# A Fourier mixing layer with a gated MLP: the second sequence chunk half plain and half by seven products, and VectorE's side work dealt out anew

## The chip, the cores and the metric

The kernel runs on 1 core of one Trainium2 chip. The metric is the device time of one execution in microseconds. Before the change it is 672.76 us, the median of 3 runs (672.74 to 672.93).

## What is computed

`x` is 2048 x 512 in fp32. Its rows are normalised, go through a discrete Fourier transform (along the hidden axis, then along the sequence, of which the real part is kept), and the result is multiplied with a gate from an MLP with 1792 hidden units.

```python
xn = _layernorm(x, axis=-1)
a = jnp.einsum("bsd,ed->bse", xn, dft_hid_re)
b = jnp.einsum("bsd,ed->bse", xn, dft_hid_im)
s = jnp.einsum("ts,bse->bte", dft_seq_re, a) - jnp.einsum("ts,bse->bte", dft_seq_im, b)
h = jnp.einsum("bsd,df->bsf", xn, w1) + b1
h = where(h > 0, h, 0) ** 2
g = silu(jnp.einsum("bsf,fd->bsd", h, w2) + b2)
out = x + s * g
```

## The kernel before

**Arithmetic.** An fp32 operand is split into a high and a low half (`split`, lines 141 to 143): ScalarE writes the high half with a copy that rounds (L136), VectorE the rest by a subtraction (L139). A product of two operands is three matmuls, in the order high x high, high x low, low x high (`PASSES`). Products of 2 x 2 blocks are made in two ways. *Plain*: eight block products, with no sums. *Seven products* (a scheme of the Strassen kind, `PRODUCTS`): seven block products, for which both operands need four sums of blocks more, and whose results are put together by seven additions (`closing_of`, on VectorE, L363, after copies by ScalarE of what lies in PSUM).

**Stages.** TensorE works through four in turn. First the sequence transform: 8 chunks of the output's columns, each a loop over 8 pairs `j` of 128 row blocks of `x`; the normalised `x` is the stationary operand (`XC[j]`), the cosine and sine tables `ct` the moving one. Then the hidden transform (Y units, `wd`), the first MLP layer (H units, `w1`), and the second with the gate and the output. A step of the first stage is one pair of one chunk, written (c, j).

**Chunks 0 and 1 are plain** (`PLAIN = 2`, `products`, lines 388 to 399): per pair 24 matmuls of 512 columns (`pq_b...` in the profile). Chunk 0 normalises `x` as it goes. Chunks 2 to 7 use seven products (`mm`, lines 377 to 384): per step 42 matmuls of 256 columns (`m`, L382), in seven banks of PSUM.

**A step's operand.** For step n, `u` is the raw table (512 KB, three buffers, loaded by SP, L293). VectorE makes four sums in it with three instructions (`sums_b`, L304 to L306); then `g`, one of two buffers, is written by the split: ScalarE's high half as soon as TensorE has finished the step before last, VectorE's low half behind it. In the code of step n stand, in this order, its matmuls, the sums of step n+2, the split of step n+1, the load of step n+4, then closings of the chunk before (`LATER`) and jobs (`EARLY`, `go`, lines 406 to 414). This is the order in which each engine gets its instructions.

**Jobs.** While the first stage runs, the engines also prepare later weights: `d0` to `d3` are the parts of `wd` (raw load into `pq00`, sums, split of 768 elements and then of 1024, each stored to DRAM), `v0`, `v1`, `v6` are parts of `w1`, `p...` are loads of prepared weights, `y...` early operands of the next stage. For the stationary side, `sums` folds the normalised `x` (four instructions of 1024 elements per half of the pairs, L275), and `split_sums` and `split_s1` split the sums into `XC`. Before, this ran beside chunk 1 (`aside`, `beside`), with a budget of 3.6 us per pair.

**The end of a chunk.** ScalarE copies product 1 and then products 7, 5 and 3 out of PSUM (`left`), so that the next chunk may use those banks; VectorE makes the first two closings at once and the others in later steps.

**Hidden units.** In an H unit ScalarE seeds regions of PSUM with negated copies (`seed`, L146), and applies bias, relu and square. For the units in `ACT_PAIR` ScalarE also does the relu and the square of the lower half (L848 and L879); for the others VectorE does it (L860 and L875).

Of the kernel before, what the change touches and what calls it, by code (L numbers as in the profile page):

```python
# [22 lines left out]
PLAIN = 2  # L23

ASIDE = 3.6

SIDE = {7: 1}
# [22 lines left out]
LATER = {0: 1, 1: 1, 2: 2, 4: 1}  # L50
# [44 lines left out]
ACT_PAIR = (4, 5, 6, 8, 10, 12, 14, 16, 18, 21, 25)  # L95
# [9 lines left out]
A11, A21, A12, A22, S2, S3, S4 = range(7)  # L105
S1 = A21

# [23 lines left out]
def fnet_gated_kernel(ctx, tc, x, xt, ct, wd, w1, w2, b1, b2, out):  # L131
# [122 lines left out]

    def ln_hi(j, h):

        nc.vector.tensor_scalar(XC[j][:, 2 * h:2 * h + 2, HI, :], halves(xr[j][:, h]), stats[:, 0, h, j:j + 1],
                                stats[:, 1, h, j:j + 1], op0=ALU.subtract, op1=ALU.mult)

    def xc_parts(j, h):  # L260
        s = slice(2 * h, 2 * h + 2)
        return XC[j][:, s, HI, :], XC[j][:, s, LO, :], halves(xn32[j][:, h])

    s1 = {}

    def sums(g):


        s = xn32[ND * g, "tile"].rearrange("p j h (b n) -> p j (h b) n", b=2)
        t = s1[g] = buf(f"pq1{g}", [P, ND, CW], f"s1_{g}")  # L270
        for to, a, b, op in ((t, s[:, :, 1], s[:, :, 3], ALU.subtract),
                             (s[:, :, 1], s[:, :, 1], s[:, :, 0], ALU.subtract),
                             (s[:, :, 0], t, s[:, :, 0], ALU.subtract),
                             (s[:, :, 2], s[:, :, 2], s[:, :, 0], ALU.add)):
            nc.vector.tensor_tensor(to, a, b, op=op)  # L275
            yield 1.2

    def split_sums(j):
        s = xn32[j].rearrange("p h (b n) -> p (h b) n", b=2)
        split(XC[j][:, S2:S4 + 1, HI, :], XC[j][:, S2:S4 + 1, LO, :], s[:, 0:3])  # L280
        return 0.9

    def split_s1(j):
        split(XC[j][:, S1, HI, :], XC[j][:, S1, LO, :], s1[j // ND][:, j % ND])
        return 0.4
# [9 lines left out]
    def plain_parts(c, j, hs=slice(0, 2)):  # L295
        if (c, j) not in part:
            part[c, j] = operand_buf("g" + "ab"[j % 2], f"g{c}_{j}", 0 if (c, j) == (PLAIN - 1, NJ - 1) else 3 if j in TURNED else 1, (2, 4, CW))
# [4 lines left out]
    def sums_b(t, r):  # L302

        nc.vector.tensor_tensor(t[:, 0:2], r[:, 0:1].to_broadcast([P, 2, 256]), r[:, 1:3], op=ALU.add)  # L304
        nc.vector.tensor_tensor(t[:, 2], t[:, 1], r[:, 1], op=ALU.add)
        nc.vector.tensor_tensor(t[:, 3], t[:, 2], r[:, 3], op=ALU.add)  # L306

    def sums_a(t, a21, a11_a22, a11, a12, turned=False):

        nc.vector.tensor_tensor(t[:, 0:2], a21.to_broadcast([P, 2, 256]), a11_a22, op=ALU.subtract)  # L310
        if turned:
# [9 lines left out]

    def sums_w1(t, r):
        sums_a(t, r[:, 0:1], r[:, 1:4:2], r[:, 1], r[:, 2], turned=True)
# [31 lines left out]
    def closing_of(part_, ms, room):  # L355
# [4 lines left out]
        for to, m, frm, op in ((C11, 2, C21, ALU.add), (C22, 6, C21, ALU.add), (C21, 7, C22, ALU.subtract),  # L360
                               (C12, 5, C22, ALU.subtract), (C22, 5, C21, ALU.add), (C12, 3, C12, ALU.add),
                               (C21, 4, C21, ALU.subtract)):
            nc.vector.tensor_tensor(part_(to), halves(room.get(m, ms[m])), part_(frm), op=op)  # L363
            yield
# [8 lines left out]
    def some(steps_, n):  # L373
        for _ in range(n):
            next(steps_)

# [9 lines left out]
    accs = [[bank(tag, f"pq0_{tag}") for tag in ("b20", "b21", "bb", "bc")]]  # L386

    def products(c, j, h):

        for passes in [PASSES] if c else [[q] for q in PASSES]:  # L390
            for k in range(ND):
                one_product(c, j, h, k, passes)

    def one_product(c, j, h, k, passes=PASSES):
        for a_, b_ in passes:
            w = XC[j][:, 2 * h + k // 2, a_, k % 2 * P:(k % 2 + 1) * P]
            nc.tensor.matmul(accs[c][k], w, part[c, j][:, b_, 2 * h:2 * h + 2],  # L397
                             start=j == 0 and h == 0 and (a_, b_) == (HI, HI),
                             stop=j == NJ - 1 and h == 1 and (a_, b_) == (LO, HI))

    one, two = slice(0, 1), slice(1, 2)
    steps = [(c, j) for c in range(PLAIN, NC) for j in range(NJ)]
    order = [(c, j) for c in range(PLAIN) for j in range(NJ)] + steps
# [12 lines left out]
    def weight(n, raw_, sums_, to, k, e=None, turn=False):  # L416

        if e:
            e = buf(e, [P, 8, 256], f"{n}rt")
            r, t = e[:, 0:4], e[:, 4:8]  # L420
        else:
            r, t = buf("pq00", [P, 4, 256], f"{n}r"), buf("pq01", [P, 4, 256], f"{n}t")
# [4 lines left out]
        sums_(t, r)  # L427
# [7 lines left out]
    makers["d"] = lambda n: weight(f"wd{n}", wd[n], sums_b, WDD[n], n % 2, "e" if n == 1 else None, True)  # L435
    makers["v"] = lambda n: weight(f"w1{n}", w1[n], sums_w1, W1D[n], 0)
# [59 lines left out]
    junk = bank("b31", "junk")  # L496
# [30 lines left out]
    for h in range(2):  # L527
        products(0, 0, h)
    def run(*names):
        go(*names)  # L530
        return 1.6

    aside = chain(sums(0), (split_sums(j) for j in range(ND)), sums(1), (split_sums(j) for j in range(ND, NJ)),
                  (run(v) for v in ("d0", "d0", "d0", "d1", "d1", "d1")))
    load_c(0, 3)
    load_x(4)
    for j in range(1, NJ):
# [27 lines left out]
        for _ in range(SIDE.get(j, 0)):  # L565
            next(aside)
        for h in range(2):
            products(0, j, h)
# [8 lines left out]
    accs.append([bank(tag, f"pq1_{tag}") for tag in ("b30", "b31", "b32", "ba")])  # L577

    def beside(spent):
        while spent < ASIDE:  # L580
            spent += next(aside, ASIDE)

# [3 lines left out]
    def plain_out(k):  # L586
        to = plain[k // 2].rearrange("p (i m d t) -> p d m i t", i=2, m=2, d=2)[:, k % 2]
        copy(to, accs[0][k].rearrange("p (m i t) -> p m i t", m=2, i=2))

    plain_out(0)  # L590
    plain_out(1)
    beside(1.5)
    plain_out(2)
    plain_out(3)
    for k in range(2):
        nc.sync.dma_start(PQD[0][:, k].rearrange("p k n -> p (k n)"), plain[k])
    for j in range(NJ - 1):
# [12 lines left out]
    step_split(0)  # L610
    step_load(3)
    split_s1(NJ - 2)
    for k in (2, 3):
        one_product(1, NJ - 1, 0, k)
    step_sums(1)
    split_s1(NJ - 1)
    for k, h in ((2, 1), (0, 0), (0, 1), (1, 0), (1, 1), (3, 1)):
        one_product(1, NJ - 1, h, k)
    last = buf("e", [P, 2048], "plain1")

    def last_out(k, op):
        to = last.rearrange("p (h i m d t) -> p h d m i t", h=2, i=2, m=2, d=2)[:, k // 2, k % 2]
        op(to, accs[1][k].rearrange("p (m i t) -> p m i t", m=2, i=2))

    for k, op in ((2, copy), (0, copy), (1, copy)):
        last_out(k, op)


    assert not list(aside)
    closing = None  # L630
    for n, s in enumerate(steps):
        c, j = s
        if j == 0:
# [20 lines left out]
        if j == NJ - 1:  # L654
            e = buf("e", [P, 2048], f"c{c}")
# [575 lines left out]
```

## Time and profile before

| what | us |
|---|---|
| median of 3 runs | 672.76 |
| the profiled execution's own time | 672.81 |
| its span, first to last instruction | 671.0 |
| TensorE (PE) busy | 665.1 (99%) |
| VectorE (DVE) busy | 596.4 (89%) |
| ScalarE (ACT) busy | 380.2 (57%) |
| matmuls of chunks 2 to 7 (L382), 2016 | 228.7 |

The granted clock of TensorE is 1.00. Rows of the timeline read: start, duration, engine, line, operation, output<-input, partitions x elements, count, and in brackets the idle time before it with what ended it. A group's row has, after the bar, busy time and the mean ns of one, then the idle time before. Durations of instructions that follow each other overlap a little at their ends, so work in a row is counted from start to start.

### The profile page before, as it was taken

How to read it: one execution, taken by the hardware profiler on the slowest of the kernel's cores; microseconds unless marked ns; L12 is line 12 of the kernel's file. 1: busy time of each engine (PE TensorE's matmuls, PEld its weight loads, DVE VectorE, ACT ScalarE, POOL GpSimd, SP SyncE). 2: the span in 40 equal slices, each digit the busy share in tenths (PEclk: the TensorE clock that was granted, in tenths of full speed). 3: DMA queues.
4: the chain of work that ended last, by engine and by line, in shares of the span. 5: the costliest groups of instructions: out<-in, count | busy, mean ns of one | idle time of the engine just before them, and what ended most of it. 6: DMA issues, size and time to landing. Idle time of an engine off the chain costs nothing.

```text
span 671.0 us, 13184 instructions
## 1 busy us (share of the span) xinstructions
PE 665.1 (99%) x5437; PEld 646.3 (96%) x5437; DVE 596.4 (89%) x831; ACT 380.2 (57%) x524; POOL 8.8 (1%) x11
## 2 busy tenths in 40 slices
PE   9999999999999999999999999999999999999997
PEld 6888889999999999999999999999999999999997
DVE  7997888999999999899899988977877889999997
ACT  6855664634445454444464557888778865454451
POOL 0000000000000000000000000000000000101010
PEclk9999999999999999999999999999999999999999
DMA  8635497646556774759588558565755866777775
GB/s 292 226 115 206 145 347 269 220 142 224 200 167 226 252 282 162 262 186 346 184 303 278 181 189 317 202 251 205 271 182 198 324 243 214 190 218 190 219 205 156
DMA packets 51739, 150.82 MB, mean 225 GB/s; under 512 B 4960, under 2 KB 19552, under 8 KB 50272
## 3 DMA queue, kind: packets, MB, share of 16 engines
q1 hardware_dynamic: 43568, 129.28, 56.9%
q10 hardware_dynamic: 6208, 18.88, 7.1%
q0 software_dynamic: 1904, 1.84, 1.9%
q8 instruction: 42, 0.69, 0.4%
q14 instruction: 17, 0.14, 0.1%
HBM read 101.98 MB, written 47.99 MB: 223 GB/s over the span
## 4 chain that ended last, share of the span: by engine, by line
PE 96%; DVE 1%; ACT 1%; DMA 0%; issue 0%; ACTq 0%; SPq 0%; DVEq 0%
PE m L382 34%; PE m_o L896 15%; PE r_B L790 13%; PE r_A L790 9%; PE pq_b L397 8%; PE r_C L790 4%; PE r_D L790 4%; PE m_last L896 4%; PE pq_ba L397 2%; PE pq_bc L397 2%; PE pq_bb L397 2%; DVE z L1146 0%; DMA x<-in_x 0%; DVE z L946 0%; ACT h L848 0%
## 5 line engine op out<-in xcount | busy, mean ns | idle before, releaser
L382 PEld LDWEIGHTS m<-g,xc 128*128 128x128 f32 x2016 | 228.6, 188 | 0.1
L382 PE MATMUL m<-g,xc 128*128 128x256 f32 x2016 | 228.7, 276 | 0.0
L136 ACT ACTIVATE g<-u 128x1792 fp32r<-128x1792 f32 (+2 forms) x65 | 99.0, 1523 | 126.9 <-PE m L382 89.0
L139 DVE TENSOR_TENSOR g<-u,g 128x1792 fp32r<-128x1792 f32 (+2 forms) x66 | 116.9, 1772 | 19.8 <-ACT g L136 19.2
L896 PE MATMUL m_o<-w,g 128*128 128x256 f32 x882 | 100.5, 276 | 0.0
L896 PEld LDWEIGHTS m_o<-w,g 128*128 128x128 f32 x882 | 100.3, 188 | 0.0
L136 ACT ACTIVATE g<-hr 128x1792 fp32r<-128x1792 f32 (+2 forms) x31 | 48.2, 1565 | 40.0 <-PE m_o L896 16.8
L790 PE MATMUL r_B<-xT,w 128*128 128x256 f32 x504 | 66.6, 277 | 0.4 <-ACT r_B L146 0.4
L397 PE MATMUL pq_b<-g,xc 128*128 128x512 f32 x240 | 65.2, 391 | 0.4 <-DVE small L247 0.4
L790 PEld LDWEIGHTS r_B<-xT,w 128*128 128x128 f32 x504 | 61.5, 188 | 0.5 <-ACT r_B L146 0.5
L139 DVE TENSOR_TENSOR g<-hr,g 128x1792 fp32r<-128x1792 f32 (+2 forms) x31 | 56.7, 1837 | 2.9 <-ACT g L136 2.8
L397 PEld LDWEIGHTS pq_b<-g,xc 128*128 128x128 f32 x240 | 44.7, 188 | 10.7 <-ACT g L136 0.8
L790 PE MATMUL r_A<-xT,w 128*128 128x256 f32 x336 | 42.8, 276 | 0.0
L790 PEld LDWEIGHTS r_A<-xT,w 128*128 128x128 f32 x336 | 40.2, 188 | 0.0
L790 PE MATMUL r_B<-wdp,yg 128*128 128x256 f32 x288 | 35.8, 277 | 0.0
L304 DVE TENSOR_TENSOR u<-u 128x512 f32<-128x512 f32 x48 | 32.8, 684 | 1.9 <-DMA u<-in_ct 1.9
L790 PEld LDWEIGHTS r_B<-wdp,yg 128*128 128x128 f32 x288 | 34.1, 188 | 0.0
L896 PE MATMUL m_last<-w,g 128*128 128x256 f32 x294 | 33.5, 276 | 0.0
L896 PEld LDWEIGHTS m_last<-w,g 128*128 128x128 f32 x294 | 33.4, 188 | 0.0
L139 DVE TENSOR_TENSOR yg<-yraw,yg 128x1792 fp32r<-128x1792 f32 x13 | 26.2, 2018 | 0.6 <-ACT yg L136 0.6
L136 ACT ACTIVATE yg<-yraw 128x1792 fp32r<-128x1792 f32 x13 | 22.2, 1708 | 5.8 <-DVE yraw L313 5.3
L790 PE MATMUL r_D<-xT,w 128*128 128x256 f32 x168 | 23.6, 276 | 0.0
(192 smaller groups left out, 877.8 us busy)
## 6 DMA issues: line engine op xcount, KB each, us to landing
u<-in_ct SPq DMA_DIRECT2D x63, 512.0 KB, 3.8
hd<-h ACTq DMA_DIRECT2D x28, 512.0 KB, 3.9
hr<-hd SPq DMA_DIRECT2D x28, 512.0 KB, 3.8
wdp<-wdd SPq DMA_DIRECT2D x8, 896.0 KB, 6.5
yraw<-pqd SPq DMA_DIRECT2D x13, 512.0 KB, 5.9
pqd<-c SPq DMA_DIRECT2D x6, 1024.0 KB, 6.3
w<-w1d SPq DMA_DIRECT2D x6, 896.0 KB, 8.2
y<-y ACTq DMA_DIRECT2D x8, 512.0 KB, 5.2
```

Of the source, the lines that this page charges most:

```text
L136: nc.scalar.activation(hi, src, AF.Copy)
L139: nc.vector.tensor_tensor(lo, src, hi.bitcast(F32), op=ALU.subtract)
L304: nc.vector.tensor_tensor(t[:, 0:2], r[:, 0:1].to_broadcast([P, 2, 256]), r[:, 1:3], op=ALU.add)
L382: nc.tensor.matmul(ps[:, d], w[:, a_, d * P:(d + 1) * P], halves(mv(b_)), start=first and d == 0 and (a_, b_) == (HI, HI), stop=last and ( ...
L397: nc.tensor.matmul(accs[c][k], w, part[c, j][:, b_, 2 * h:2 * h + 2], start=j == 0 and h == 0 and (a_, b_) == (HI, HI), stop=j == NJ - 1 a ...
L790: nc.tensor.matmul(self.region(REGION[k]), w, mv, start=i == 0 and k in (1, 7), stop=i == len(ops) - 1, skip_group_check=True)
L896: nc.tensor.matmul(m[:, i * 256:(i + 1) * 256], ready[n][:, a_, H_SLOT[a], i * P:(i + 1) * P], W2[p][:, b_, b], start=p == 0 and i == 0 an ...
```

## The change

Chunk 1 becomes mixed. Its pairs 4 to 7 come first, plain: eight products of 256 columns per pair, added up in four banks, three of which are those of products 2, 4 and 3, and a fourth bank, `Z`. Pairs 0 to 3 follow with seven products into the same banks. One closing is added for `Z` (L371 of the new file, `z`). The sums of `x` are made in place, with four blocks split by one instruction; the slots of `XC` move so that A21, which becomes S1, lies beside the others. The sums for pairs 4 to 7 are split behind steps (1,1), (1,2), (2,0) and (2,1) (`SUMS_AT`). `d0` to `d3`, which ran from chunk 1 to chunk 2, run from the mixed part to chunk 4, and the jobs behind them follow; a weight's three sums are now two jobs instead of one. Closings come one per step. The hidden unit 5 leaves `ACT_PAIR`.

```diff
-PLAIN = 2
-ASIDE = 3.6
-SIDE = {7: 1}
+MIXED = 4, 5, 6, 7
+SUMS_AT = {1: 4, 2: 5, 4: 6, 5: 7}
...
 EARLY = {
-    (2, 0): ("d2",), (2, 1): ("d2",), (2, 2): ("d3",), (2, 4): ("d3",), (2, 5): ("d3",), (2, 6): ("d3",),
...
+    (2, 2): ("d0",), (2, 4): ("d0", "d1"), (2, 5): ("d1",), (2, 6): ("d1",),
...
-LATER = {0: 1, 1: 1, 2: 2, 4: 1}
+LATER = {0: 1, 1: 1, 2: 1, 3: 1, 4: 1}
+LATER_1 = {0: 1, 1: 1, 2: 1, 3: 1, 4: 1, 5: 1}
...
-ACT_PAIR = (4, 5, 6, 8, 10, 12, 14, 16, 18, 21, 25)
+ACT_PAIR = (4, 6, 8, 10, 12, 14, 16, 18, 21, 25)
...
-A11, A21, A12, A22, S2, S3, S4 = range(7)
+A11, A12, A22, S2, S3, S4, A21 = range(7)
...
     def split_sums(j):
         s = xn32[j].rearrange("p h (b n) -> p (h b) n", b=2)
-        split(XC[j][:, S2:S4 + 1, HI, :], XC[j][:, S2:S4 + 1, LO, :], s[:, 0:3])
-        return 0.9
-    def split_s1(j):
-        split(XC[j][:, S1, HI, :], XC[j][:, S1, LO, :], s1[j // ND][:, j % ND])
+        split(XC[j][:, S2:S1 + 1, HI, :], XC[j][:, S2:S1 + 1, LO, :], s)
...
+    def plain_step(j):
+        g = part.pop((1, j))
+        for k, pairs_ in ((2, ((A11, 1), (A12, 3))), (4, ((A21, 1), (A22, 3))), (3, ((A11, 0), (A12, 2))),
+                          (Z, ((A21, 0), (A22, 2)))):
+            if k not in ms:
+                ms[k] = bank("ba" if k == Z else banks(1)[k], f"m{k}_1")
+            for i, (a, q) in enumerate(pairs_):
+                mm(ms[k], XC[j][:, a], lambda b_: g[:, b_, q], j == MIXED[0] and not i, k == Z and j == MIXED[-1] and i == 1)
...
-    steps = [(c, j) for c in range(PLAIN, NC) for j in range(NJ)]
+    steps = [(1, j) for j in range(NJ) if j not in MIXED] + [(c, j) for c in range(2, NC) for j in range(NJ)]
...
+    for i, j in enumerate(MIXED):
...
+        elif i == 2:
+            split(*plain_parts(1, MIXED[3]))
+            split_sums(3)
+            some(side[1], 1)
+            step_sums(0)
+            go("d0", "d0")
+        else:
+            step_sums(1)
+            step_split(0)
+            some(side[1], 1)
+        plain_step(j)
+        load_c(*order[NJ + i + 4])
...
-            if j == max(LATER):
+            if j == max(LATER_1):
                 nc.sync.dma_start(PQD[c - 1].rearrange("p h k n -> p (h k n)"), e)
```

**Where instructions move.** First, VectorE ahead of the first step with seven products. `g` are the operands, named by chunk and pair (`g1_7` is chunk 1, pair 7), `u` the tables, `xn32_4` the `x` of pairs 4 to 7, `xc3` a pair's stationary operand, `wd0t` sums of a weight. Before, that step is (2,0), and between the split for the last plain pair and the split for it stands:

```order
L139 TENSOR_TENSOR g1_7_799<-u1_7_681,g1_7_799 128x1024
L304 TENSOR_TENSOR u2_0_725<-u2_0_725 128x512
L305 TENSOR_TENSOR u2_0_725<-u2_0_725 128x256
L306 TENSOR_TENSOR u2_0_725<-u2_0_725 128x256
L304 TENSOR_TENSOR wd2t_720<-wd2r_719 128x512
L305 TENSOR_TENSOR wd2t_720<-wd2t_720,wd2r_719 128x256
L306 TENSOR_TENSOR wd2t_720<-wd2t_720,wd2r_719 128x256
L139 TENSOR_TENSOR xc5_123<-s1_1_640,xc5_123 128x256
L139 TENSOR_TENSOR wd1g_795<-wd1rt_574,wd1g_795 128x1024
L139 TENSOR_TENSOR g2_0_840<-u2_0_725,g2_0_840 128x1792
```

After, it is (1,0), right behind the split for plain pair 7 (`g1_7`):

```order
L140 TENSOR_TENSOR xc3_128<-xn32_0_184,xc3_128 128x4x256
L274 TENSOR_TENSOR xn32_4_374<-xn32_4_374 128x4x256
L301 TENSOR_TENSOR u1_0_619<-u1_0_619 128x512
L303 TENSOR_TENSOR u1_0_619<-u1_0_619 128x256
L304 TENSOR_TENSOR u1_0_619<-u1_0_619 128x256
L301 TENSOR_TENSOR wd0t_630<-wd0r_629 128x512
L303 TENSOR_TENSOR wd0t_630<-wd0t_630,wd0r_629 128x256
L304 TENSOR_TENSOR wd0t_630<-wd0t_630,wd0r_629 128x256
L301 TENSOR_TENSOR u1_1_680<-u1_1_680 128x512
L303 TENSOR_TENSOR u1_1_680<-u1_1_680 128x256
L304 TENSOR_TENSOR u1_1_680<-u1_1_680 128x256
L140 TENSOR_TENSOR g1_0_748<-u1_0_619,g1_0_748 128x1792
```

A third set of three sums now stands ahead of the split (that of step (1,1), which before was made behind it), and a split and a fold of 1024 elements take the place of the weight's.

Second, VectorE at the end of chunk 3, from the split for (4,0) to that for (4,1); `c3` is the chunk's result, `m` its products in PSUM, `wd2g` a split weight. Before:

```order
L139 TENSOR_TENSOR g4_0_1745<-u4_0_1589,g4_0_1745 128x1792
L363 TENSOR_TENSOR c3_1750<-m2_3_1325,c3_1750 128x2x256
L363 TENSOR_TENSOR c3_1750<-m6_3_1326,c3_1750 128x2x256
L304 TENSOR_TENSOR u4_2_1695<-u4_2_1695 128x512
L305 TENSOR_TENSOR u4_2_1695<-u4_2_1695 128x256
L306 TENSOR_TENSOR u4_2_1695<-u4_2_1695 128x256
L139 TENSOR_TENSOR g4_1_1811<-u4_1_1641,g4_1_1811 128x1792
```

After:

```order
L140 TENSOR_TENSOR g4_0_1893<-u4_0_1738,g4_0_1893 128x1792
L374 TENSOR_TENSOR c3_1898<-m2_3_1468,c3_1898 128x2x256
L374 TENSOR_TENSOR c3_1898<-m6_3_1469,c3_1898 128x2x256
L140 TENSOR_TENSOR wd2g_1844<-wd2t_1635,wd2g_1844 128x1024
L301 TENSOR_TENSOR u4_2_1842<-u4_2_1842 128x512
L303 TENSOR_TENSOR u4_2_1842<-u4_2_1842 128x256
L304 TENSOR_TENSOR u4_2_1842<-u4_2_1842 128x256
L140 TENSOR_TENSOR g4_1_1965<-u4_1_1791,g4_1_1965 128x1792
```

A weight's split has come in between the closings and the sums. ScalarE's half of it stands, in the new order, behind the three copies of `left` and ahead of the next `g`:

```order
L137 ACTIVATE g4_0_1893<-u4_0_1738 128x1792
L147 ACTIVATE c3_1898<-m1_3_1467 128x2x256
L147 ACTIVATE left3_1899<-m7_3_1472 128x512
L147 ACTIVATE left3_1899<-m5_3_1471 128x512
L147 ACTIVATE left3_3_1900<-m3_3_1470 128x512
L137 ACTIVATE wd2g_1844<-wd2t_1635 128x1024
L137 ACTIVATE g4_1_1965<-u4_1_1791 128x1792
```

Before, nothing stood there between the third copy and that `g`.

Third, SP's transfers from the load for (5,0) to that for (5,2). Before:

```order
L293 DMA u5_0_2024<-in_ct 128x1024
L652 DMA pqd3_78<-c3_1750 128x2048
L293 DMA u5_1_2076<-in_ct 128x1024
L432 DMA w1d1_88<-w11g_2078 256x1x768
L293 DMA u5_2_2130<-in_ct 128x1024
```

After:

```order
L287 DMA u5_0_2176<-in_ct 128x1024
L451 DMA wdd3_86<-wd3g_2179 256x1x768
L287 DMA u5_1_2231<-in_ct 128x1024
L658 DMA pqd3_78<-c3_1898 128x2048
L451 DMA wdd3_86<-wd3g_2179 256x1x1024
L439 DMA w10r_2237<-in_w1 128x1024
L287 DMA u5_2_2288<-in_ct 128x1024
```

The chunk's store, a weight's store and a raw load now stand together between two loads of `u`.

More of the change, by code (lines that the diff above doesn't have):

```diff
@@ L527, in fnet_gated_kernel @@
     for h in range(2):
[L528 to L534, printed above, removed]
+        products(0, h)
+    side = sums(0), sums(1)
     load_c(0, 3)
@@ L564, in fnet_gated_kernel @@
         split_lo(*xc_parts(j, 1))
[L565 to L566 removed]
+        if j == NJ - 1:
+            next(side[0])
         for h in range(2):
[L568 removed]
+            products(j, h)
         g = plain_parts(*order[j + 1])
@@ L630, in fnet_gated_kernel @@
+    LAST = {(c, max(j for c_, j in steps if c_ == c)) for c in range(1, NC)}
     closing = None
```

193 lines of the change are left out of this document (93 added, 100 removed), and 9 rows, old and new, of the table EARLY.

## The prediction

> **What bounds the kernel now.** I read the page first, then TensorE's waits and timeline, then VectorE's and ScalarE's timelines between 50 and 330 us, where the change lies. The page's engine line and two groups of matmuls:
>
> ```profile
> PE 665.1 (99%) x5437; PEld 646.3 (96%) x5437; DVE 596.4 (89%) x831; ACT 380.2 (57%) x524; POOL 8.8 (1%) x11
> ...
> L382 PE MATMUL m<-g,xc 128*128 128x256 f32 x2016 | 228.7, 276 | 0.0
> L397 PE MATMUL pq_b<-g,xc 128*128 128x512 f32 x240 | 65.2, 391 | 0.4 <-DVE small L247 0.4
> ```
>
> TensorE never rests, so time is its work plus any wait that appears. TensorE's timeline at the start and the end of chunk 1:
>
> ```profile
> 50.95 2.20 PE L397 MATMUL pq_b<-g,xc 128*128 128x512 f32 x9
> ...
> 83.63 2.20 PE L397 MATMUL pq_b<-g,xc 128*128 128x512 f32 x9
> ...
> 86.35 2.20 PE L397 MATMUL pq_b<-g,xc 128*128 128x512 f32 x9
> ...
> 94.67 15.59 PE L382 MATMUL m<-g,xc 128*128 128x256 f32 x136
> ```
>
> Twelve wide matmuls take 86.35 - 83.63 = 2.72 us, 0.227 each; a narrow one takes 228.7/2016 = 0.1134, just half. So a plain pair (24 wide or 48 narrow) costs 5.44 us, and a seven-product step (42 narrow) 4.76.
>
> Its one wait between the start and the tail is in hidden unit 5; ScalarE's rows there, then TensorE's:
>
> ```profile
> 431.37 0.73 ACT L848 ACTIVATE h<-h,b1s 128x512 f32<-128x512 f32 x1
> 432.13 1.06 ACT L879 ACTIVATE h<-h 128x1024 f32<-128x1024 f32 x1
> 433.60 0.37 ACT L146 ACTIVATE r_B<-r_A 128x256 f32<-128x256 f32 x1 [0.40 <-ACT h L879]
> ```
>
> ```profile
> 432.82 0.84 PE L790 MATMUL r_D<-xT,w 128*128 128x256 f32 x6
> 434.02 1.66 PE L790 MATMUL r_B<-xT,w 128*128 128x256 f32 x12 [0.35 <-ACT r_B L146]
> ```
>
> Six narrow matmuls from 432.82 end at 433.50, but the next start at 434.02, so 0.52 is lost; that is 0.05 after the copy that they wait for (433.60 + 0.37), the time of a signal.
>
> **The clock that VectorE must keep.** For each step ScalarE writes the high half of g when the step before last has freed its buffer, VectorE the low half. ScalarE's row and VectorE's, then VectorE's through a step with a job in it:
>
> ```profile
> 109.21 1.71 ACT L136 ACTIVATE g<-u 128x1792 fp32r<-128x1792 f32 x1 [3.05 <-PE m L382]
> ```
>
> ```profile
> 110.95 2.02 DVE L139 TENSOR_TENSOR g<-u,g 128x1792 fp32r<-128x1792 f32 x1 [1.21 <-ACT g L136]
> ```
>
> ```profile
> 149.03 2.03 DVE L139 TENSOR_TENSOR g<-u,g 128x1792 fp32r<-128x1792 f32 x1
> 150.97 0.68 DVE L310 TENSOR_TENSOR w10t<-w10r 128x512 f32<-128x512 f32 x1
> ...
> 152.49 0.68 DVE L304 TENSOR_TENSOR u<-u 128x512 f32<-128x512 f32 x1
> ...
> 154.01 2.02 DVE L139 TENSOR_TENSOR g<-u,g 128x1792 fp32r<-128x1792 f32 x1
> 155.95 0.68 DVE L363 TENSOR_TENSOR c<-m,c 128x512 f32<-128x512 f32 x1
> 156.55 0.68 DVE L304 TENSOR_TENSOR u<-u 128x512 f32<-128x512 f32 x1
> ```
>
> From start to start: low half 1.94, a set of three sums 1.52, one closing 0.60. Each step needs 1.94 + 1.52 = 3.46, which leaves 4.76 - 3.46 = 1.30 for jobs. Where nothing makes VectorE late, the low half ends at 110.95 + 2.02 = 112.97. The next step starts at 94.67 + 4 x 4.76 = 113.71; its second matmul, 0.11 later, is the first to read the low half. With 0.05 for the signal, VectorE has 0.80 us in reserve. That is my rule: each step changes the reserve by 1.30 minus its jobs, never above 0.80, and TensorE waits for what goes below zero.
>
> The other jobs, from VectorE's timeline of chunk 1:
>
> ```profile
> 64.12 1.22 DVE L139 TENSOR_TENSOR g<-u,g 128x1024 fp32r<-128x1024 f32 x1
> 65.26 0.42 DVE L139 TENSOR_TENSOR xc<-s,xc 128x256 fp32r<-128x256 f32 x1
> ...
> 77.01 0.95 DVE L139 TENSOR_TENSOR wd0g<-wd0r,wd0g 128x768 fp32r<-128x768 f32 x1
> 77.88 1.22 DVE L139 TENSOR_TENSOR wd0g<-wd0t,wd0g 128x1024 fp32r<-128x1024 f32 x1
> ```
>
> Start to start, 1024 elements take 1.14, 768 take 0.87.
>
> **The change, part by part.**
>
> *Matmuls.* Chunk 1 goes from 192 wide to 4 x 48 + 4 x 42 = 360 narrow: 43.52 us become 40.80, **-2.72**. Between 86.35 and 94.67 there are 36 wide ones, 8.16 us of work in 8.32: the scattered last pair loses 0.16, and it goes, **-0.16** (at least nothing, if the new order loses as much). [...]
>
> *ScalarE's pair in the hidden layer.* The rows of unit 5 stand above; VectorE's around unit 6:
>
> ```profile
> 437.83 0.48 DVE L860 SCALAR_TENSOR_TENSOR h<-r_B,b1s,h 128x256 f32<-128x256 f32 x1 [1.72 <-PE r_B L790]
> 438.96 0.69 DVE L875 SCALAR_TENSOR_TENSOR h<-h 128x512 f32<-128x512 f32 x1
> ```
>
> Without the 0.73 and with half the square, the copy of r_B is some 1.1 us earlier and the lost 0.52 comes back: **-0.52** (nothing, if something else is late there). VectorE gets one op of 0.69 and two that are 0.06 longer; its idle 1.72 at 437.83 hides them, else they cost 0.8.
>
> *VectorE before the first seven-product step, (1,0).* Rows of ScalarE, in chunk 1 and at the end of chunk 2:
>
> ```profile
> 83.83 1.06 ACT L136 ACTIVATE g<-u 128x1024 fp32r<-128x1024 f32 x1 [2.67 <-PE pq_ba L397]
> ...
> 130.92 1.96 ACT L146 ACTIVATE left<-m 128x512 f32<-128x512 f32 x3 [0.48 <-PE m L382]
> 133.01 1.71 ACT L136 ACTIVATE g<-u 128x1792 fp32r<-128x1792 f32 x1
> ```
>
> ScalarE starts on g 0.20 after its buffer is free (83.63 to 83.83). After the change, g1_7's is free at 50.95 + 2 x 5.44 = 61.83, its high half done at 62.03 + 1.06 = 63.09. VectorE then has, by the order, three ops of 1.14 and three sets of sums, 7.98 us, to 71.07; the low half of g1_0 ends at 73.09. TensorE wants it at 50.95 + 4 x 5.44 + 0.11 - 0.05 = 72.77: **+0.32**, and the reserve is zero.
>
> *The steps behind it.* Jobs of 1.14 (a fold, or a split of x's sums) in four steps raise the reserve to 0.64; two closings, 1.20, to 0.74. Then 1.14 + 0.60 takes it to 0.30, the same again to -0.14, and 0.87 + 0.60 costs 0.17: **+0.31**, at (2,3) and (2,4). Later a closing with 1.14 and a small transposition leaves 0.14 at (2,6), so nothing. Before, the jobs were lumped but fewer, since chunk 1 had no sums and no closings: none of these waits was there. I take what the sums give; the bounds are zero and, if every thin reserve of this chain breaks by as much again, 1.3.
>
> *End of chunk 3.* The second half of wd2's split now stands behind the closings, and on ScalarE behind the three copies of left. Put on the end of chunk 2, which has the same copies: its last step began at 94.67 + 7 x 4.76 = 127.99; the copies end at 132.88, ScalarE's half of the split, 1.06, at 133.94. VectorE, held there with sums and g behind it, goes on at 135.08, ends the sums at 136.60 and the low half at 138.62. TensorE wants that at 127.99 + 9.52 + 0.06 = 137.57: **+1.05** at (4,1). At the end of chunk 4 two sums of a set (0.80) stand there: 0.80 + 1.30 - 2.00 leaves 0.10.
>
> *ScalarE* loses three copies and gains four bigger splits; at 57% with waits of 3 us for TensorE it has room.
>
> Sum: 2.72 + 0.16 + 0.52 - 0.32 - 0.31 - 1.05 = 1.72 us gained. The profiled execution took 672.81, its span 671.0, the median of the runs is 672.76: 671.0 us after.
>
> **The rivals.** About 0.2%, 1.35 us, is what a measurement of this kernel can tell from no change.
>
> *VectorE keeps up* (0.17). No wait at (1,0) to (4,1), if a job is done earlier than its place in the row suggests: 669.4. Without the wait at (4,1) alone: 670.0. Against it: engines take their rows in order, as 110.95's wait for ScalarE shows with the sums of the next step queued behind it.
>
> *The gain is given back* (0.20). A second wait like (4,1)'s, at (5,1) with its 0.10 of reserve, and the thin steps (0.14 to 0.30) breaking by some 0.3: 671.0 + 1.3 = 672.3.
>
> *The loads of u come late* (0.10); the other side. Transfers and landing times in the page, and u's between 255 and 300 us:
>
> ```profile
> pqd<-c SPq DMA_DIRECT2D x6, 1024.0 KB, 6.3
> wdd<-wd0g SPq DMA_DIRECT2D x1, 1024.0 KB, 9.0
> ```
>
> ```profile
> DMA to landing us min/median/max: 3.3/4.0/6.4
> ```
>
> At (4,5), and again at (6,5), the chunk's store, a weight's store and a load, 2.5 MB, now stand between two loads of u. A load of u is issued when one low half is done, and TensorE feels it if it lands later than 2 x 4.76 - 1.94 - 1.52 + 0.80 = 6.86 us after. The slowest seen is 6.4. If two take the 9.0 of the slowest store, that is 2 x 2.1 = 4.3 us: 675.3. It turns to slower by 0.2% from 8.4 us on. For it: beside other transfers a load already takes 6.4 instead of 4.0. Against: TensorE did not wait even then. [...]
>
> *Narrow matmuls cost more than half of a wide one* (0.01). By the mean of one, 276 against 391 ns, chunk 1 would grow by 360 x 276 - 192 x 391 = 24.3 us, to about 698. Against: 2016 x 276 ns is 556 us, and they took 228.7. [...]
>
> **How the numbers follow.** The forecast has 0.52: 671.0, with the bounds of its terms 670.4 (no waits but (4,1)'s) to 671.7 (no 0.16, no 0.52), nine tenths of it under 671.4. Faster: 0.47 + 0.17 = 0.64. Same: 0.05 + 0.20 = 0.25. Slower: 0.10 + 0.01 = 0.11. The range leaves out the slow rivals and the edges of the others: 669.6 to 672.9.
>
> **What would show it.** Chunk 1's matmuls end 2.9 us earlier less 0.3; TensorE waits for VectorE's g near 73, 106, 111 and 174 us, about 0.3, 0.1, 0.2 and 1.05 us; the wait for r_B near 434 is gone. No such waits, or a total of 669.4, would prove VectorE's chain wrong; a VectorE wait for u of over 2 us near 207 or 283 the DMA part; matmuls of chunk 1 that don't start every 0.113 us the first term.

## The result and the profile after

The changed kernel takes 711.59 us, median of 4 runs (708.35 to 713.53), against 672.85 of the kernel before, median of 4 (672.74 to 673.15): ratio 1.057, interval 1.0527 to 1.0613. The forecast was 671.0. The profiled execution took 712.77, its span is 711.0, 40.0 longer than before. The page's lines of engines and of the narrow matmuls:

```profile
PE 678.2 (95%) x5605; PEld 664.3 (93%) x5605; DVE 608.3 (86%) x844; ACT 381.4 (54%) x516; POOL 8.8 (1%) x11
...
L389 PE MATMUL m<-g,xc 128*128 128x256 f32 x2376 | 285.2, 283 | 23.0 <-DVE g L140 21.6
```

TensorE, which had no idle time worth a row here before, now waits 23.0 us among the narrow matmuls (256 columns, chunks 1 to 7), and these are busy 285.2 us where 2376 x 0.1134 = 269.4 would do. Its timeline, the rows that begin with a wait (in brackets: how long, and for whom):

```profile
73.98 53.43 PE L389 MATMUL m<-g,xc 128*128 128x256 f32 x461 [0.19 <-DVE g L140]
128.50 0.38 PE L389 MATMUL m<-g,xc 128*128 128x256 f32 x1 [1.09 <-ACT g L137]
131.09 31.48 PE L389 MATMUL m<-g,xc 128*128 128x256 f32 x251 [2.21 <-DVE g L140]
...
165.49 19.96 PE L389 MATMUL m<-g,xc 128*128 128x256 f32 x168 [2.21 <-DVE g L140]
186.03 34.15 PE L389 MATMUL m<-g,xc 128*128 128x256 f32 x294 [0.58 <-DVE g L140]
226.12 30.55 PE L389 MATMUL m<-g,xc 128*128 128x256 f32 x252 [5.94 <-DVE g L140]
259.39 25.69 PE L389 MATMUL m<-g,xc 128*128 128x256 f32 x210 [2.72 <-DVE g L140]
287.75 26.27 PE L389 MATMUL m<-g,xc 128*128 128x256 f32 x210 [2.67 <-DVE g L140]
319.08 40.90 PE L389 MATMUL m<-g,xc 128*128 128x256 f32 x335 [5.05 <-DVE g L140]
361.22 1.65 PE L797 MATMUL r_A<-wdp,yg 128*128 128x256 f32 x12 [1.24 <-ACT c L147]
365.42 1.66 PE L797 MATMUL r_B<-wdp,yg 128*128 128x256 f32 x12 [1.19 <-ACT r_B L147]
371.38 1.63 PE L797 MATMUL r_B<-wdp,yg 128*128 128x256 f32 x12 [0.22 <-DVE y L807]
```

The first and that at 186.03 are waits that the prediction has (at (1,0) and at (4,1)), at half their size. The long ones stand where it has none. What held VectorE, from its waits between 44 and 345 us (total, times, longest):

```profile
DVE w10t L311 <- DMA w10r<-in_w: 7.5, 1, 7.5
DVE yt L311 <- DMA yr<-pqd: 6.1, 1, 6.1
DVE wd1t L301 <- ACT wd1r L147: 4.6, 1, 4.6
DVE wd2t L301 <- ACT wd2r L147: 3.4, 1, 3.4
DVE w11t L311 <- DMA w11r<-in_w: 3.3, 1, 3.3
DVE w16t L311 <- DMA w16r<-in_w: 3.2, 1, 3.2
```

Six waits, 28.1 us together, and each is the first sum of a weight (or of the first y) waiting for the raw data that it adds up. For wd1 and wd2 the name is ScalarE's, whose sign change stands between: ScalarE's own waits, between 44 and 375 us, show the load behind it (their first row is another wait, for a chunk's store, and is taken up below).

```profile
ACT c L147 <- DMA pqd<-c: 8.8, 2, 7.4
...
ACT wd1r L147 <- DMA wd1r<-in_wd: 6.9, 1, 6.9
ACT wd2r L147 <- DMA wd2r<-in_wd: 5.8, 1, 5.8
```

Not one of VectorE's waits here is for u. Of the seven raw loads of wd1 to wd3, the parts of w1 and the first y, only wd3's costs VectorE no wait (ScalarE waits 2.1 us for it): the change issues it at (3,7) and adds it up at (4,1), two steps later; the six others are added up one step after their issue. The place of the longest, (4,5), on SP's queue and on VectorE:

```profile
210.22 0.42 SPq L658 DMA_DIRECT2D pqd<-c  x1
210.97 0.53 SPq L451 DMA_DIRECT2D wdd<-wd3g  x1
211.53 1.91 SPq L439 DMA_DIRECT2D w10r<-in_w  x1
```

```profile
221.92 0.69 DVE L311 TENSOR_TENSOR w10t<-w10r 128x512 f32<-128x512 f32 x1 [7.51 <-DMA w10r<-in_w]
222.53 0.68 DVE L301 TENSOR_TENSOR u<-u 128x512 f32<-128x512 f32 x1
```

VectorE was free for the sum at 221.92 - 7.51 = 214.41, 2.9 us after the load's issue. Transfers issued between 205 and 225 us, with the time from issue to landing at the end of the row:

```profile
w10r<-in_w SPq DMA_DIRECT2D x1, 512.0 KB, 10.4
```

10.4 - 2.9 = 7.5: the wait. In the kernel before, the same load was issued at 141.94 with no store ahead of it in its step, landed 4.3 us later, and the first sum came 9.0 us after the issue (150.97, a row of the prediction):

```profile
w10r<-in_w SPq DMA_DIRECT2D x1, 512.0 KB, 4.3
```

While VectorE waits, the next u sums and the low half of g stand behind that sum in its row (222.53), and TensorE waits for g: 5.94 of the 7.51, the rest is reserve and the room of a step.

The waits are not the whole loss: behind them the granted clock is lower. Stretches of 2 us around this wait, with the columns from, to, length, busy us (instructions) of PE, PEld, DVE, ACT and POOL, the granted clock, the DMA engines' share and GB/s:

```profile
222.00:224.00 2.00, 0.00 (x0) 0.00 (x0) 1.93 (x4) 0.00 (x0) 0.00 (x0) 0.58 0.02 8
...
226.00:228.00 2.00, 1.88 (x9) 1.88 (x10) 1.97 (x6) 0.00 (x0) 0.00 (x0) 0.50 0.42 106
228.00:230.00 2.00, 2.00 (x14) 2.00 (x14) 1.93 (x5) 0.00 (x0) 0.00 (x0) 0.71 0.39 156
230.00:232.00 2.00, 2.00 (x19) 2.00 (x19) 2.00 (x2) 0.00 (x0) 0.00 (x0) 1.00 0.00 0
```

The clock falls to 0.50 during the wait and stays there for some 3 us of work: 9 matmuls in the first 2 us instead of 19; from 230 us on it is 1.00 again. TensorE stopped at 226.12 - 5.94 = 220.18; the mean is 1.00 from 220 to 222 and 0.58 from 222 to 224, which puts the fall, by estimate, near 222.3, after 2.1 us of idling.

### The profile page after: what moved, and what is told of

Read it like the earlier page. It is cut to its first block, busy times and chain, and to the rows that moved or that the text cites. A ratio compares the mean times of both kernels' runs of the same rounds, so it can differ in the third digit from the quotient of the medians.

```text
span 711.0 us, 13521 instructions
## 1 busy us (share of the span) xinstructions
PE 678.2 (95%) x5605; PEld 664.3 (93%) x5605; DVE 608.3 (86%) x844; ACT 381.4 (54%) x516; POOL 8.8 (1%) x11
## 4 chain that ended last, share of the span: by engine, by line
PE 66%; DVE 19%; DMA 9%; ACT 3%; issue 1%; SPq 1%; ACTq 0%; DVEq 0%
PE m L389 15%; PE m_o L903 14%; PE r_B L797 12%; PE r_A L797 8%; DVE g L140 7%; PE pq_b L400 4%; PE r_C L797 4%; PE r_D L797 4%; PE m_last L903 3%; DVE u L301 2%; DVE c L374 2%; ACT g L137 2%; DVE u L303 1%; DMA w10r<-in_w 1%; DMA pqd<-c 1%
## 5 line engine op out<-in xcount | busy, mean ns | idle before, releaser
L389 PE MATMUL m<-g,xc 128*128 128x256 f32 x2376 | 285.2, 283 | 23.0 <-DVE g L140 21.6
L389 PEld LDWEIGHTS m<-g,xc 128*128 128x128 f32 x2376 | 283.1, 194 | 25.2 <-DVE g L140 23.2
L137 ACT ACTIVATE g<-u 128x1792 fp32r<-128x1792 f32 (+2 forms) x65 | 101.4, 1560 | 151.8 <-PE m L389 92.6
L140 DVE TENSOR_TENSOR g<-u,g 128x1792 fp32r<-128x1792 f32 (+2 forms) x66 | 120.0, 1819 | 18.6 <-ACT g L137 18.5
L400 PE MATMUL pq_b<-g,xc 128*128 128x512 f32 x144 | 41.3, 392 | 1.9 <-DVE small L248 1.9
L301 DVE TENSOR_TENSOR u<-u 128x512 f32<-128x512 f32 x52 | 35.6, 684 | 0.0
L400 PEld LDWEIGHTS pq_b<-g,xc 128*128 128x128 f32 x144 | 26.7, 188 | 8.6 <-ACT g L137 2.7
L797 PE MATMUL r_A<-wdp,yg 128*128 128x256 f32 x192 | 23.7, 277 | 1.2 <-ACT c L147 1.2
```

Source lines behind the costliest of these rows:

```text
L137: nc.scalar.activation(hi, src, AF.Copy)
L140: nc.vector.tensor_tensor(lo, src, hi.bitcast(F32), op=ALU.subtract)
L389: nc.tensor.matmul(ps[:, d], w[:, a_, d * P:(d + 1) * P], halves(mv(b_)), start=first and d == 0 and (a_, b_) == (HI, HI), stop=last and ( ...
L400: nc.tensor.matmul(accs[k], w, part[0, j][:, b_, 2 * h:2 * h + 2], start=j == 0 and h == 0 and (a_, b_) == (HI, HI), stop=j == NJ - 1 and ...
L797: nc.tensor.matmul(self.region(REGION[k]), w, mv, start=i == 0 and k in (1, 7), stop=i == len(ops) - 1, skip_group_check=True)
```

## The experiments

Line numbers shift by a few between kernels: the narrow matmuls are L389 in the changed kernel, L387 in those derived from it, L381 and L382 in those derived from the one before.

**Raw loads a step earlier.** The changed kernel with six loads issued one step earlier (not in the lines shown: v1 at (5,2), v6 at (5,7) and y1 at (6,4)), and the buffer of the sums is taken when the sums start, so that the load need not wait for the last split of the weight before. Nothing else moves.

```diff
-    (2, 2): ("d0",), (2, 4): ("d0", "d1"), (2, 5): ("d1",), (2, 6): ("d1",),
-    (3, 0): ("d1",), (3, 2): ("d1", "d2"), (3, 3): ("d2",), (3, 4): ("d2",), (3, 6): ("d2",), (3, 7): ("d2", "d3"),
-    (4, 1): ("d3",), (4, 2): ("d3",), (4, 4): ("d3",), (4, 5): ("d3", "v0"), (4, 6): ("v0",), (4, 7): ("v0",),
...
+    (2, 2): ("d0",), (2, 3): ("d1",), (2, 4): ("d0",), (2, 5): ("d1",), (2, 6): ("d1",),
+    (3, 0): ("d1",), (3, 1): ("d2",), (3, 2): ("d1",), (3, 3): ("d2",), (3, 4): ("d2",), (3, 6): ("d2",), (3, 7): ("d2", "d3",),
+    (4, 1): ("d3",), (4, 2): ("d3",), (4, 4): ("d3", "v0",), (4, 5): ("d3",), (4, 6): ("v0",), (4, 7): ("v0",),
...
-        r, t = buf("pq00", [P, 4, 256], f"{n}r"), buf("pq01", [P, 4, 256], f"{n}t")
+        r = buf("pq00", [P, 4, 256], f"{n}r")
         nc.sync.dma_start(r, raw_)
         yield
+        t = buf("pq01", [P, 4, 256], f"{n}t")
```

> The changed kernel with one thing moved: the raw loads of five weights' and one early operand's jobs (wd1, wd2, three parts of w1, the y operand) are issued one step earlier, so that two steps and not one lie between a load and the first sum that reads it. Theory L (VectorE, whose instructions run in order, stands still for a raw load that was issued too late, and everything behind it is late): VectorE's waits of 3.2 to 7.5 us for these loads go, with them TensorE's waits of 2 to 6 us and the half clock after each; 670.5 to 673 us. Rival O (VectorE has too much work per step, and its waits for loads are only where it shows): TensorE's waits stay, 700 us or more. Rival C (the stores of the weights fill the DMA engines): a load takes 6 us wherever it is issued, about half of the waits stay, 685 to 695.

Measured: 680.23 us (678.56 to 680.97) against 673.15, ratio 1.0102 (1.0087 to 1.0117). About 31 of the 39 us are back. TensorE's waits among the narrow matmuls, and their group:

```profile
73.82 101.73 PE L387 MATMUL m<-g,xc 128*128 128x256 f32 x882 [0.19 <-DVE g L138]
176.34 38.55 PE L387 MATMUL m<-g,xc 128*128 128x256 f32 x336 [0.80 <-DVE g L138]
215.12 76.61 PE L387 MATMUL m<-g,xc 128*128 128x256 f32 x672 [0.22 <-DVE g L138]
292.41 35.14 PE L387 MATMUL m<-g,xc 128*128 128x256 f32 x293 [0.68 <-DVE g L138]
```

```profile
L387 PE MATMUL m<-g,xc 128*128 128x256 f32 x2376 | 274.0, 277 | 2.0 <-DVE g L138 1.9
```

All six waits for raw data are gone but for 0.2 at y's. So the loads are the cause of the long waits. It stays 7 us above the kernel before, more than this theory allowed, and two things of it are to be explained. Its clock is 0.999, yet the matmuls are busy 274.0 instead of 269.4; that is taken up below. And VectorE now waits for loads of u, five times and 3.5 us together; the 1.16 of them near 289 us stands ahead of the low half for which TensorE waits 0.68. (The kernel before has two such waits, 1.20 and 0.69, and TensorE felt neither.)

**The same step, the load ahead of the store.** Here the loads stay in their step, but are issued ahead of the second split and its store; so at (2,4), (3,2), (4,5), (5,3), (6,0) and (6,5).

```diff
-    (2, 2): ("d0",), (2, 4): ("d0", "d1"), (2, 5): ("d1",), (2, 6): ("d1",),
+    (2, 2): ("d0",), (2, 4): ("d1", "d0"), (2, 5): ("d1",), (2, 6): ("d1",),
...
```

> The changed kernel with the raw load issued in the same step as before the edit, one step ahead of its first sum, but ahead of the split and of the store of the weight before it, not behind them. Theory L, in the form that the place behind the split and its store of 1 MB costs the time (about 1.9 us on SP's row and 1.8 us of landing): the waits shrink from 3.3 us to under 1, 672 to 678 us. In the form that one step is too short in any case: waits of 2 us and more stay, 690 us or more. Rival O: unchanged, 705 to 713.

Measured: 686.93 us (685.45 to 688.26), ratio 1.0204 (1.0188 to 1.0221), between the two forms that were expected. VectorE still waits 4.0 for w10 and 3.7 for y, and the load of w10 lands after 7.6 us; with a step more ahead it landed after 6.3:

```profile
w10r<-in_w SPq DMA_DIRECT2D x1, 512.0 KB, 7.6
```

The store of its own weight is only a part: at (4,5) the chunk's 1 MB store is issued ahead of the load in either order. Three kernels with one place give 10.4, 7.6 and 6.3 us for a load that takes 4.3 with no store ahead of it in its step; the prediction had no row for that. Whether the load waits behind the stores or is drawn out beside them, these landing times do not show.

**One late load in the kernel before.** The load of v1 moved to (3,6), right behind v0's last store, and its sums to (3,7): the changed kernel's pattern once, in the kernel before.

```diff
-    (3, 1): ("v0",), (3, 3): ("v0",), (3, 5): ("v0",), (3, 6): ("v0",),
-    (4, 1): ("v1",), (4, 3): ("v1",), (4, 5): ("v1",), (4, 6): ("v1",),
+    (3, 1): ("v0",), (3, 3): ("v0",), (3, 5): ("v0",), (3, 6): ("v0", "v1",), (3, 7): ("v1",),
+    (4, 5): ("v1",), (4, 6): ("v1",),
```

> The kernel before with one cause put in: the raw load of the second prepared part of w1 stands right behind the second split and store of the first part, and its sums one step later, at the end of chunk 3; nothing else. Theory L: VectorE waits 2 to 3 us for that load, TensorE about 2.8 us near 180 us, and the clock is at half for some 3 us after; 676 to 679 us in place of 672.8. Rival O: VectorE has room here, so 672.8, within 0.5.

Measured: 678.9 us (678.31 to 679.74), ratio 1.0087 (1.0071 to 1.0102), as the theory has it. The load lands after 7.2 us. One wait of VectorE, one of TensorE and one fall of the clock (to 0.62 from 180 to 182 us and 0.53 from 182 to 184) cost 6 us:

```profile
175.25 0.69 DVE L309 TENSOR_TENSOR w11t<-w11r 128x512 f32<-128x512 f32 x1 [3.00 <-DMA w11r<-in_w]
```

```profile
180.37 149.43 PE L381 MATMUL m<-g,xc 128*128 128x256 f32 x1301 [3.54 <-DVE g L138]
```

**VectorE late without any load.** The kernel before with 4, 7 and 11 idle operations of VectorE behind three steps: this prices a wait of TensorE by its length.

```diff
         go(*EARLY.get(s, ()))
+        for _ in range({(3, 4): 4, (4, 4): 7, (5, 4): 11}.get(s, 0)):
+            nc.vector.tensor_tensor(b2s, b2s, b2s, op=ALU.max)
```

> The kernel before with useless work for VectorE (maxima of the bias tile with itself, 0.72 us each, which leave its values as they are) behind steps (3,4), (4,4) and (5,4): 4, 7 and 11 of them, 2.9, 5.0 and 7.9 us. By the reserve rule a step with one closing takes 1.5 us of it without a wait, so TensorE waits 1.4, 3.5 and 6.4 us, 11.3 in all. If a wait costs its length alone: 684.1 us and a granted clock of 1.00. If the clock falls to half for some 3 us after a wait of over 2 us, each such wait costs 1.5 to 3 us more: 687 to 691 us, with half clock behind the second and third wait and none behind the first.

Measured: 690.49 us (689.96 to 691.54), ratio 1.0259 (1.0242 to 1.0276). TensorE's waits are 1.32, 3.50 and 6.40, 11.2 together; the time is 17.3 longer. Behind the second (206 us) and the third the clock is at 0.50, behind the first at 1.00:

```profile
208.00:210.00 2.00, 2.00 (x11) 2.00 (x11) 2.00 (x3) 0.00 (x0) 0.00 (x0) 0.50 0.96 378
```

So the six us beyond the waits (17.3 - 11.2) need no late load and no change of order: it is what these waits cost TensorE afterwards.

**Unit 5 alone.** The kernel before with one edit of the change.

```diff
-ACT_PAIR = (4, 5, 6, 8, 10, 12, 14, 16, 18, 21, 25)
+ACT_PAIR = (4, 6, 8, 10, 12, 14, 16, 18, 21, 25)
```

> The kernel before, with hidden unit 5 taken from ACT_PAIR and nothing else changed. The prediction's term says -0.52 us: the wait of 0.35 for the copy of r_B near 434 us is gone, 672.3. The rival (VectorE is late there in its place): no change, 672.8. Over 673.5 would say that VectorE's pair costs more than it gives back.

Measured: 672.68 us (672.2 to 673.45, 11 runs) against 673.11 (21 runs), ratio 0.9995 (0.9986 to 1.0003). TensorE's wait for r_B is gone from its waits. The difference of 0.43 fits the term, but the interval holds no change too. And the trace shows a new loss. VectorE's operations for the lower half now stand ahead of its split of `xT`, the next rows of x, and TensorE's weight load waits for that split:

```profile
430.64 0.69 DVE L875 SCALAR_TENSOR_TENSOR h<-h 128x512 f32<-128x512 f32 x1
431.25 0.95 DVE L139 TENSOR_TENSOR xT<-xr,xT 128x768 fp32r<-128x768 f32 x1
...
432.25 0.30 PEld L790 LDWEIGHTS r_A<-xT,w 128*128 128x128 f32 x2 [0.23 <-DVE xT L139]
```

The 12 matmuls of r_A from 430.92 take 1.68 us to the next start, the same 12 in the kernel before 1.36; the changed kernel has this gap too (470.27 to 471.95). Over the whole stretch (428.74 to 436.88 before, 429.56 to 437.37 here) 0.33 us come back.

**The chunk's store at its own end.** The first experiment's kernel, with the store of chunks 3 to 7 in the step of the last closing again; the change had put it one step later for every chunk.

```diff
-            if j == max(LATER_1):
+            if j == max(LATER_1 if c == 2 else LATER):
```

> The first experiment's kernel (raw loads ahead, 680.2 us), and the store of a chunk's result issued in the step of its last closing: the fifth step of chunks 3 to 7, as in the kernel before, not the sixth. In the first experiment's trace ScalarE waits 0.81, 1.28 and 5.84 us with the first copy of the next chunk's result (207, 285 and 326 us), whose buffer that store still reads. Theory (the store is the wait behind the 0.68 at 291.7 and the 0.79 at 331): ScalarE's three waits and TensorE's two are gone, with the slower spacing of matmuls behind them; 677.5 to 679. Rival (ScalarE's wait is for TensorE, as its last name in the trace says, and the u loads alone make the 0.68): the wait at 326 stays, 679.5 to 680.5.

Measured: 680.47 us (678.4 to 681.18), ratio 1.0101 (1.0085 to 1.0118): no gain on 680.23, against my expectation. The three waits of ScalarE for that store and TensorE's two in the y stage did go. But one step earlier the 1 MB stands ahead of the raw loads of v0 and y1, and VectorE waits for these again:

```profile
DVE yt L309 <- DMA yr<-pqd: 2.7, 1, 2.7
DVE w10t L309 <- DMA w10r<-in_w: 1.7, 1, 1.7
```

The y wait makes TensorE wait 2.06 at 288.95, and the clock falls (0.50 from 290 to 292 us). What the store gave back, the load behind it took.

**The same edit in the kernel before, the other way round.** Its store one step later, and nothing else.

```diff
-            if j == max(LATER):
+            if j == max(LATER) + 1:
```

> The kernel before, with the store of each chunk's result issued one step later (the sixth step, as in the changed kernel), and nothing else. Theory: ScalarE's first copy of the next result waits for that store, which still reads the same buffer; with a landing of 6 to 9 us it is free just about when the copy is due, so chunks 3 to 6 show 0 to 1.3 us of ScalarE waiting that TensorE does not feel, but at the end of chunk 7 TensorE waits about 0.8 to 1.2 for the copy of r_B, as in the changed kernel: 673.5 to 674.5, ratio 1.001 to 1.002. Rival (the changed kernel's waits near 361 us come from its late loads alone): no change, 673.1.

Measured: 675.25 us (674.24 to 675.69, 7 runs) against 672.86 (12 runs), ratio 1.0029 (1.0018 to 1.004): more than expected. TensorE's two waits below are 1.09 of the 2.4 us; what makes up the rest is not shown. ScalarE's first copies of the results of chunks 6 and 7, and TensorE behind the second:

```profile
284.02 0.60 ACT L146 ACTIVATE c<-m 128x512 f32<-128x512 f32 x1 [1.26 <-DMA pqd<-c]
322.55 0.60 ACT L146 ACTIVATE c<-m 128x512 f32<-128x512 f32 x1 [5.24 <-DMA pqd<-c]
```

```profile
327.40 1.67 PE L790 MATMUL r_B<-wdp,yg 128*128 128x256 f32 x12 [0.87 <-ACT r_B L146]
...
333.37 1.67 PE L790 MATMUL r_B<-wdp,yg 128*128 128x256 f32 x12 [0.22 <-DVE y L800]
```

The buffer of the next result is still being read by the store. These are the changed kernel's waits at 365.42 and 371.38, so they belong to the later store, not to the late loads.

**Jobs placed anew.** Store at its own end, loads a step ahead, and VectorE's jobs moved to where the first experiment's trace has room: sums of x's second group into the hole near 56 us, the splits of x's sums a step earlier, wd2's splits away from the end of chunk 3, v0's second sum away from the end of chunk 4, v0's and y1's loads ahead of the chunk's store.

```diff
-SUMS_AT = {1: 4, 2: 5, 4: 6, 5: 7}
+SUMS_AT = {0: 4, 1: 5, 2: 6, 4: 7}
...
-    (4, 1): ("d3",), (4, 2): ("d3",), (4, 4): ("d3", "v0",), (4, 5): ("d3",), (4, 6): ("v0",), (4, 7): ("v0",),
+    (4, 1): ("d3",), (4, 2): ("d3",), (4, 3): ("d3", "v0",), (4, 5): ("d3",), (4, 6): ("v0",),
...
             split_sums(0)
+            some(side[1], 2)
             plain_out(2)
```

> The kernel above, and VectorE's work moved where the first experiment's trace has room: two of the four sums of x's second group into the 2.36 us in which VectorE waits for ScalarE near 56 us, the splits of x's sums one step earlier, wd2's two splits one step earlier (away from the end of chunk 3), the second sum of v0 one step later (away from the end of chunk 4), v0's and y1's loads a step ahead of the chunk's store. Theory (TensorE's remaining waits are VectorE's lateness by the reserve rule, each with a stretch of 118 ns spacing behind it): the waits at 73.8, 106.9, 175.5, 214.9, 291.7 go, and some 79 us at 118 ns with them; 670.5 to 672.5, below the kernel before by 0.5 to 2. Rival (the spacing of 118 ns is not brought on by waits, but by what VectorE and the transfers do beside TensorE): the waits go but stretches of 118 ns stay, 674 to 677. If a wait for a load appears in another place, its length and place are in VectorE's waits.

Measured: 672.07 us (670.0 to 673.05, 11 runs) against 673.11 (21 runs), ratio 0.9979 (0.997 to 0.9989). Two waits of 0.2 are left, at 73.67 and 278.82.

**Two waits less.** The last sums of x's second group ahead of the low half of g1_7, and y1's first split one step later.

```diff
             split_sums(2)
-            some(side[1], 1)
+            some(side[1], 2)
...
             split_sums(3)
-            some(side[1], 1)
...
-    (7, 0): ("p0",), (7, 1): ("y1", "p3",), (7, 2): ("p3",), (7, 3): ("y1", "y0", "p2",), (7, 4): ("y2", "p2",), (7, 5): ("y0", "y0",), (7, 6): ("y0",), (7, 7): ("y2", "y2", "y2",),
+    (7, 0): ("p0",), (7, 1): ("p3",), (7, 2): ("y1", "p3",), (7, 3): ("y1", "y0", "p2",), (7, 4): ("y2", "p2",), (7, 5): ("y0", "y0",), (7, 6): ("y0",), (7, 7): ("y2", "y2", "y2",),
```

> The kernel with the jobs placed anew (672.07 us, 0.9979 of before), and two edits for what its trace still shows: the last two sums of x's second group both stand ahead of the low half of g1_7 (the chain from there to the low half of g1_0, which makes TensorE wait 0.19 at 73.7, is one sum of 1.14 shorter), and the first split of y1 stands one step later, behind the low half that loads of u made late at 290 us. Theory: the wait at 73.7 goes, and the stretch of 118 ns spacing from 298 to 323 us (25 us x 0.0046/0.118 = 1.0) with the short wait that starts it: 670.5 to 671.5. Rival (the stretch has another trigger): 671.8 to 672.2.

Measured: 671.39 us (670.19 to 672.69, 6 runs) against 672.86 (12 runs), ratio 0.9974 (0.9962 to 0.9985). The profiled execution took 670.19, its span is 668.3. No wait is left in the mixed stage:

```profile
L387 PE MATMUL m<-g,xc 128*128 128x256 f32 x2376 | 269.7, 276 | 0.0
```

This is the change with its order of jobs mended, and it beats both kernels, the one before by 0.15 to 0.38%.

## Why the prediction was wrong

**The step that failed** is the reserve rule, "each step changes the reserve by 1.30 minus its jobs". It counts a job as work only. A job's first sum also waits for its raw load, and the change brings these two from two steps apart or more to one, with 1 to 2 MB of stores ahead of the load in the queue. The limit that the prediction should have set is in its own rows: the load is issued behind one low half, the sum stands near the next, so it has some 3 us (2.9 measured) and not the 6.86 of a load of u; even 4.0, the usual landing of u, is over that. The 9.0 us of a weight's store was quoted as well. Applied to the raw loads it gives some 6 us of waiting at (4,5) alone, over three times the whole gain; six such places gave 28.1 us on VectorE and the long waits of TensorE.

**The price of a wait** was the second omission: the rule charges what goes below zero and nothing after. In the changed kernel the 2376 matmuls are busy 285.2 us, in the last experiment 269.7, so 15.5 us came after the waits. In the first experiment, at a clock of 0.999, the same difference is 274.0 - 269.7 = 4.3: that much goes at full clock to a slower spacing (last section) and to the restarts behind waits (in the changed kernel a lone matmul behind one, at 128.50, is busy 0.38, where in a row each takes 0.1134). If the changed kernel loses as much in this way, some 11 of the 15.5 are left for the halved clock; this is an estimate.

The span's 40.0 us, then: 23.0 of waits and 15.5 behind them in the mixed stage, 1.24 + 1.19 + 0.22 in the y stage, 0.8 in chunk 0 (its last pair ends at 51.74 instead of 50.95; the kernel with unit 5 alone, whose chunk 0 is that of before, is 0.8 later at the y stage, so this need not come from the change), less 2.72, 0.16 and the 0.33 of unit 5, is 38.7; 1.3 are left over, which no row here places.

**Matmuls, -2.72 and -0.16: right.** 269.7/2376 is 0.1135, half of a wide one, at the new places too. From chunk 1's first matmul to the y stage the last experiment takes 320.79 - 51.21 = 269.58 us, the kernel before 323.16 - 50.95 = 272.21: 2.63 of the 2.88.

**Unit 5, -0.52: the wait is gone, but only 0.33 came back.** The prediction let VectorE's idle 1.72 hide its added work; it missed that the split of `xT` stands behind that work, and TensorE loses 0.32 there. By the medians the edit alone gave 0.43, with no change inside the interval.

**(1,0), +0.32: right place, 0.19.** That it is this chain was shown by taking one sum out of it: the wait went. In the kernel with jobs placed anew, where sums were moved but the chain behind g1_7 kept its length, it stayed at 0.19.

**(2,3) and (2,4), +0.31: too high.** In the first experiment the timeline has no wait there. Two starts at 107 us, at (2,3), lie 0.175 apart instead of 0.113. But the slower spacing of the last section begins there, which the prediction had at nothing.

**(4,1), +1.05: right place, 0.58 in the changed kernel, 0.80 in the first experiment.** With wd2's splits a step earlier it is gone.

**The rivals.** "The gain is given back" named (5,1): 0.22 in the first experiment, real and small. "The loads of u come late" named (4,5) and (6,5), the chunk's store, a weight's store and a load in one step, and both are places of long waits, 5.94 and 5.05. But it followed the wrong transfer: in the changed kernel VectorE never waits for u. That a load behind the step's stores lands late was right (10.4 us at (4,5) against 4.3), but the victim was the third transfer of the step and not the one behind it. With the raw loads out of the way, in the first experiment, u does come late at both places, but VectorE waits 0.34 to 0.42 for it (205 to 221 us) and 1.16 and 1.18 (289 and 294 us), not the over 2 us that the prediction named as the sign. "VectorE keeps up", 669.4 for no wait at all, is what the last experiment built: its profiled execution took 670.19.

**Left out** was also that the chunk's store moves one step for all chunks, while the first copy of the next result needs the buffer that it reads. Alone this costs 2.4 us in the kernel before, where ScalarE's first copy of chunk 7's result waits 5.24 us for the store.

## What to carry to other kernels

For every job in an engine's row, set the time from the issue of its load to its first use against the landing time of such a load behind the stores that share its step; a job that waits for data holds up what is queued behind it (of VectorE's 7.51 us at (4,5), TensorE felt 5.94). In these runs a wait of TensorE that brought the clock down cost some 2 to 3 us more than its length (5.8 for 3.54 with one late load, 17.3 for 11.2 with VectorE late), and short ones cost more than their length too (2.0 us of them came with 4.3 more in the first experiment). Here a store one step later made the next copy into its buffer wait 5.24 us, and one step earlier it made VectorE wait 1.7 and 2.7 for the raw loads behind it, so look at both ends.

## What the hardware showed beside

**The fall of the clock and the length of the wait.** The clock fell behind a wait of 2.06 us in one kernel (the store at its own end, 288.95), but not behind one of 2.21 that followed 0.33 in the changed kernel (165.49):

```profile
290.00:292.00 2.00, 2.00 (x11) 2.00 (x11) 1.93 (x5) 0.00 (x0) 0.00 (x0) 0.50 0.83 331
```

```profile
166.00:168.00 2.00, 2.00 (x20) 2.00 (x20) 1.90 (x6) 0.00 (x0) 0.00 (x0) 1.00 0.56 195
```

So in these runs the length of the last wait alone does not decide; what else does is not shown.

**A slower spacing at full clock.** After some waits, and after the short gap at 107 us, matmuls of the first experiment start every 0.118 us instead of 0.1134, with the granted clock at 1.00: for some 4 us behind the wait of 0.22 (19 starts in 2 us instead of 20, 216 to 220), for 35 us from 107 to 142. Stretches of 10 us with the narrow matmuls alone:

```profile
84.00:94.00 10.00, 10.00 (x90) 10.00 (x90) 1.28 (x2) 2.38 (x4) 1.00 0.34 118
...
114.00:124.00 10.00, 10.00 (x87) 10.00 (x86) 0.68 (x1) 0.00 (x0) 1.00 0.79 273
...
144.00:154.00 10.00, 10.00 (x91) 10.00 (x90) 0.00 (x0) 0.00 (x0) 1.00 0.75 261
```

A stretch also counts the matmul that reaches into it (0.28 long), so 87 of them are (10 + 0.28)/87 = 0.118 apart. The DMA share, 0.79 against 0.75 in the last two rows, does not set them apart. In the last experiment, without waits, such stretches are all but gone from the mixed stage (269.7 us for the 2376 matmuls, 0.1135 each). What ends them, and why one gap brings 4 us of them and another 35, stays open: no run here was made for it.
